# Landmark attention and two MLPs on one core: q by token parity, scores as eight 64x32 tiles, k and v in one product, and a new prologue order

## The chip, the core and the metric

The kernel runs on one core of one Trainium2 chip. The metric is the device time of the whole program in microseconds (us), the median of three runs. Engines are named as in the profile: PE (TensorE), DVE (VectorE), ACT (ScalarE), POOL (GpSimd) and SP (SyncE, which issues nearly all the loads and stores).

## What is computed

```python
a = softmax(phi, axis=2)                      # phi: 4 x 8 x 576 x 32
k_m = einsum('bhsm,bhsd->bhmd', a, k)         # 32 landmarks per head
v_m = einsum('bhsm,bhsd->bhmd', a, v)
attn = softmax(q @ k_m.T / 8)                 # 576 x 32 per head
x = (attn @ v_m), heads side by side          # 2304 tokens x 512
h = max(x @ w1, x @ w2, x @ w3)               # d_ff 768
x = h @ w_out
out = softplus(x @ m_in) @ m_out              # d_ff 2048, result 2304 x 512
```

q, k, v and phi are float32. The six weight matrices arrive as 64-bit words that the kernel turns into float32 itself.

## The kernel before

**Units.** The attention is done in eight units of one batch and four heads each (`units`); unit u has batch u // 2 and heads 0 to 3 or 4 to 7. A batch has 576 tokens, taken as four blocks of 128 and a remainder of 64 (`R4`, `SREM`). Units 0 to 3 belong to the first two batches and are worked off in the prologue; units 4 to 7 are worked off later, between the large products of the first two batches.

**The steps of a unit.** `load_phi`, `load_x` (k is i = 0, v is i = 1) and `load_q` bring the data in. `att_max` finds the largest phi of each landmark: three maxima on DVE, a product with the identity on PE that turns the 128x128 result, a row maximum, a diagonal matrix `md` and a product with ones that spreads it to all partitions. `att_exp` subtracts and exponentiates (`et`). `att_x` multiplies `et` with k or with v, for four heads side by side in four 128x32 tiles, and, the first time, `et` with a column of ones, which gives the sums of the softmax; `ri` is their reciprocal and `kvd` the normalised result. `att_tr` turns `kvd` by two products with a selection matrix (`pick2`), giving `kT` or the unit's part of v. `att_q` turns q with transposes on PE. `att_sc` multiplies `kT` with `qT`: for each half of the tokens (288 columns) two 128x64 tiles, the contraction running over two heads' 64 dimensions each. `att_sm0`, `att_sm1`, `att_sm2` and `att_fin` do the softmax over the landmarks on DVE, POOL and ACT, and split the result into a high and a low part (`ah`, `al`).

**The first MLP.** v_m and the three weight matrices are multiplied ahead (`u_step`, `u_mm`, `u_mr`: `uh`, `ul`), so that `m1_step` goes from attention weights to the maximum directly: 18 products of 288 columns for one block of 128 hidden units, one batch and one half of its tokens. `m1out` then multiplies with w_out. The weights w1 to w3 come in halves (`w_load`, three loads of 256 KB each) and are converted by `ca_step` or `conv`. All this is done for the first two batches and again for the last two; the second MLP (`m2in`, `m2out`) follows, and `m2out` writes rows of the result from SP.

**What sets the order.** The prologue's order is the hand-made list `PLAN`: each entry names a step and a unit, every step is a generator that is advanced by one `yield` per entry, and the engines keep the order of the list (`tc.manual_schedule`). After the plan a scheduler places the steps of `phase_a` and `phase_o`, and those of units 4 to 7 between them, by the slots in `C`. Each engine and SP's queue of transfers works in its order; a transfer whose buffer is still in use holds all transfers behind it on SP.

Of the kernel before, what the change touches and what calls it, by code (L numbers as in the profile page):

```python
# [68 lines left out]
    'us0': 1,  # L69
    'us1': 0,  # L70
# [3 lines left out]
def fused_kernel(ctx: ExitStack, tc: tile.TileContext, q, k, v, phi, w1, w2, w3, w_out, m_in, m_out, out):  # L74
# [63 lines left out]
    ones = const.tile([P, 2], F32, name="ones")  # L138
# [94 lines left out]

    def load_phi(u):
# [9 lines left out]
        nc.gpsimd.memset(ph[SREM:P, :, R4, :], 0.0)  # L244
        U[u]["ph"] = ph

    def load_x(u, i):
# [3 lines left out]
        if u in (2, 3):  # L251
            x = h_p.tile([P, 4, R4, D], F32, tag=f"h{2 * u - 1 - i}", name="kvm")
        else:
            x = t_p.tile([P, 4, R4, D], F32, tag=f"x{i}", name="kvm", bufs=2)
        if u in (2, 3):
            xr = wo_p.tile([SREM, 4, D], F32, tag=f"woh{2 * u - 2 + i}", name="kvr")
        else:
            xr = t_p.tile([SREM, 4, D], F32, tag=f"xr{i}", name="kvr", bufs=2)
# [5 lines left out]
    def load_q(u):  # L264
# [717 lines left out]
```

## Time and profile before

| | us |
|---|---|
| median of three runs (lowest, highest) | 730.91 (728.87, 731.75) |
| the profiled execution, whole | 731.49 |
| its span, first to last instruction | 729.7 |
| PE busy in the span | 699.0 (96%) |
| DVE, ACT, POOL busy | 410.7, 297.3, 250.9 |
| mean granted clock of PE | 0.986 of full speed |

The time to predict is that of the whole execution. PE is the busiest engine; what it does not work, and what it works at the lower of its two clock levels, stands mostly in the first 100 us, where the loads are also densest. A matmul's own duration in the trace includes the time in which the next ones already run, so what a group of matmuls costs PE is read from the start of its first to the start of what follows.

### The profile page before, as it was taken

What the parts mean: (1) busy time and instruction counts of PE and PEld (TensorE: products, weight loads), DVE (VectorE), ACT (ScalarE), POOL (GpSimd) and SP (SyncE); (2) the same over time, 40 slices, a digit from 0 to 9 for tenths busy, and PEclk for the clock granted to TensorE, in tenths of its full rate; (3) what the DMA queues carried; (4) which work ended last, traced back from release to release, by engine and by line L of the source; (5) the groups of instructions that cost most, each with busy time, mean ns of one, the idle gap of its engine ahead of it and who ended that gap; (6) DMA issues with size and microseconds to landing.
All of it is one profiled execution on the core that took longest, in us unless ns stands there. A gap on an engine that the chain in (4) does not pass through costs nothing. (4 is left out here: it accounts for less than half of the span.)

```text
span 729.7 us, 12242 instructions
## 1 busy us (share of the span) xinstructions
PE 699.0 (96%) x4680; PEld 614.9 (84%) x4680; DVE 410.7 (56%) x780; ACT 297.3 (41%) x628; POOL 250.9 (34%) x239
## 2 busy tenths in 40 slices
PE   6789999999979999989999999999999999999997
PEld 4466777888879999889988989989889899889895
DVE  4777885825689955772332685334783335333342
ACT  3454564437377734553233553222542224222221
POOL 1201233237384406842222452222542224222221
PEclk9889999999989999999999999999999999999999
DMA  8987975411234102530000231000340000011112
GB/s 194 260 266 213 284 215 163 121 33 51 69 99 142 50 1 78 152 118 1 1 0 1 59 116 57 1 1 0 90 143 1 0 1 1 0 44 44 44 49 81
DMA packets 70490, 59.25 MB, mean 81 GB/s; under 512 B 27936, under 2 KB 65312, under 8 KB 70432
## 3 DMA queue, kind: packets, MB, share of 16 engines
q1 hardware_dynamic: 70432, 58.47, 27.7%
q8 instruction: 37, 0.61, 0.3%
q14 instruction: 21, 0.17, 0.1%
HBM read 53.74 MB, written 4.72 MB: 80 GB/s over the span
## 5 line engine op out<-in xcount | busy, mean ns | idle before, releaser
L161 POOL TENSOR_TENSOR gl<-m,gh 128x384 fp32r<-128x384 f32 x96 | 100.5, 1048 | 253.7 <-ACT gh L153 237.6
L889 DVE TENSOR_SCALAR e<-pst 128x384 int32<-128x384 int32 x96 | 53.2, 555 | 134.4 <-PE pst L883 134.4
L891 ACT ACTIVATE L<-e 128x384 f32<-128x384 f32 x96 | 50.3, 524 | 184.8 <-DVE e L889 184.7
L915 PE MATMUL acc<-oh,gh 128*128 128x512 f32 x288 | 113.7, 395 | 0.4 <-ACT gh L153 0.4
L915 PE MATMUL acc<-ol,gh 128*128 128x512 f32 x288 | 113.4, 394 | 0.0
L883 PE MATMUL pst<-yb,ih 128*128 128x384 f32 x384 | 102.1, 336 | 0.0
L606 PE MATMUL psm<-ah,uh 128*128 128x288 f32 x288 | 89.9, 312 | 5.0 <-ACT mt L613 3.2
L606 PE MATMUL psm<-al,uh 128*128 128x288 f32 x288 | 86.8, 301 | 0.0
L606 PE MATMUL psm<-ah,ul 128*128 128x288 f32 x288 | 86.2, 301 | 0.3 <-DVE ul L562 0.3
L893 DVE SCALAR_TENSOR_TENSOR m<-pst,L 128x384 f32<-128x384 f32 x96 | 53.4, 556 | 55.9 <-ACT L L891 55.9
L915 PE MATMUL acc<-oh,gl 128*128 128x512 f32 x288 | 82.7, 394 | 0.0
L153 ACT ACTIVATE gh<-m 128x384 fp32r<-128x384 f32 x96 | 50.0, 523 | 63.4 <-DVE m L893 62.0
L883 PEld LDWEIGHTS pst<-yb,ih 128*128 128x128 f32 x384 | 70.0, 188 | 3.4 <-DVE m L893 0.7
L883 PE MATMUL pst<-y0h,ih 128*128 128x384 f32 x192 | 64.9, 338 | 2.7 <-DVE m L893 2.5
L606 PEld LDWEIGHTS psm<-ah,uh 128*128 128x128 f32 x288 | 55.7, 193 | 13.2 <-ACT mt L613 4.0
L883 PE MATMUL pst<-y0l,ih 128*128 128x384 f32 x192 | 64.5, 336 | 0.0
L883 PE MATMUL pst<-y0h,il 128*128 128x384 f32 x192 | 64.4, 336 | 0.0
L883 PE MATMUL pst<-yb,il 128*128 128x384 f32 x192 | 64.4, 335 | 0.0
L915 PEld LDWEIGHTS acc<-oh,gl 128*128 128x128 f32 x288 | 53.6, 187 | 11.4
L915 PEld LDWEIGHTS acc<-oh,gh 128*128 128x128 f32 x288 | 53.9, 187 | 10.5 <-ACT gh L153 0.9
L915 PEld LDWEIGHTS acc<-ol,gh 128*128 128x128 f32 x288 | 54.0, 187 | 8.9
L606 PEld LDWEIGHTS psm<-ah,ul 128*128 128x128 f32 x288 | 55.5, 193 | 1.2 <-issue 0.6
(152 smaller groups left out, 1323.1 us busy)
## 6 DMA issues: line engine op xcount, KB each, us to landing
wraw<-in_moe_w_dram SPq DMA_DIRECT2D x66, 256.0 KB, 3.8
raw<-in_moe_w_in_dram SPq DMA_DIRECT2D x16, 512.0 KB, 3.7
raw<-in_moe_w_out_dram SPq DMA_DIRECT2D x16, 512.0 KB, 3.7
out_dram<-o SPq DMA_DIRECT2D x18, 256.0 KB, 2.1
kvm<-in_k_dram SPq DMA_DIRECT2D x8, 512.0 KB, 5.3
kvm<-in_v_dram SPq DMA_DIRECT2D x8, 512.0 KB, 6.5
wor<-in_moe_w_out_dram SPq DMA_DIRECT2D x6, 512.0 KB, 3.7
ph<-in_phi_dram SPq DMA_DIRECT2D x8, 256.0 KB, 4.1
```

What stands on the lines that cost most here:

```text
L153: nc.scalar.activation(out=dst, in_=src, func=AF.Copy)
L161: return e.tensor_tensor(out=dst, in0=src, in1=hi, op=ALU.subtract)
L606: nc.tensor.matmul(x, l[:, t, ws], r[:, cs], start=(n == 0), stop=(n == 5))
L883: nc.tensor.matmul(hx, l[:, ds], r[:, cs], start=(n == 0), stop=(n == 3 * ND - 1))
L889: nc.vector.tensor_scalar(out=e.bitcast(I32), in0=hx.bitcast(I32), scalar1=0x7FFFFFFF, scalar2=None, op0=ALU.bitwise_and)
L891: nc.scalar.activation(out=L, in_=e, func=AF.Softplus, scale=-1.0)
L893: nc.vector.scalar_tensor_tensor(out=m, in0=hx, scalar=0.0, in1=L, op0=ALU.max, op1=ALU.add)
L915: nc.tensor.matmul(acc[0][t], l[:, t * P:(t + 1) * P], r, **kw)
```

## The change

The tokens of a batch are reordered: `qT` holds the even tokens of a block in partitions 0 to 63 and the odd ones in 64 to 127, so that q can be loaded in runs of four tokens (1 KB) in place of one (256 B), and so that the scores of a head have a contraction of 64. The result's rows are put back by the stores. `par` holds 1 or 0 by the parity of the head, and 1 in its last two columns; `ri` times `par` puts a head's v into the half of `kvd` that it belongs to, and one transpose then turns it. In units 4 to 7 k and v are one product (`att_x` with i = 2, 128 columns). The padding of phi and of the remainders makes all contractions 128 deep. Beside this, `PLAN` is a new list with nearly the same steps, and weight halves (1,0), (1,1), (2,0) and (3,1) get load buffers of their own.

```diff
@@ tiles and loads
-    pick2 = const.tile([P, 2, P], F32, name="pick2")
+    par = const.tile([P, 4], F32, name="par")
-        nc.gpsimd.memset(ph[SREM:P, :, R4, :], 0.0)
+        nc.gpsimd.memset(ph[SREM:P, :, R4, :], -3e38)
+        nc.gpsimd.memset(xr[SREM:P], 0.0)
@@ load_q
+        dma(out=x, in_=q[b, hs, 0:R4 * P, :].rearrange("h (p r) d -> p h (r d)", r=R4))
         for h in range(4):
-            dma(out=x[:, h // 2, :, (h % 2) * D:(h % 2 + 1) * D],
-                in_=q[b, 4 * g + h, 0:R4 * P, :].rearrange("(r p) d -> p r d", r=R4))
-        dma(out=xr, in_=q[b, hs, R4 * P:S, :].rearrange("h p d -> p h d"))
+            dma(nc.scalar if u in C["aq"] else nc.sync, out=xr[32 * h:32 * h + 32],
+                in_=q[b, 4 * g + h, R4 * P:S, :].rearrange("(p r) d -> p (r d)", r=2))
@@ att_max
-        nc.vector.tensor_tensor(out=m2, in0=ph[:, :, 0:2], in1=ph[:, :, 2:4], op=ALU.max)
-        nc.vector.tensor_tensor(out=mx, in0=m2[:, :, 0], in1=m2[:, :, 1], op=ALU.max)
-        nc.vector.tensor_tensor(out=mx[0:SREM], in0=mx[0:SREM], in1=ph[0:SREM, :, R4], op=ALU.max)
+        nc.vector.tensor_reduce(out=mx, in_=d["ph"].rearrange("p h r m -> p h m r"), op=ALU.max, axis=AX.X)
-        nc.tensor.matmul(st[:, 0:P], mx.rearrange("p h m -> p (h m)"), ident, start=True, stop=True)
+        nc.tensor.transpose(st[:, 0:P], mx.rearrange("p h m -> p (h m)"), ident)
+        if u < 4:
+            nc.scalar.activation(out=md, in_=ident, func=AF.Copy, scale=mc)
@@ att_exp
+        nc.gpsimd.tensor_tensor(out=es, in0=et[:, 0:2], in1=et[:, 2:4], op=ALU.add)
+        nc.gpsimd.tensor_tensor(out=es[:, 0], in0=es[:, 0], in1=es[:, 1], op=ALU.add)
+        nc.gpsimd.tensor_tensor(out=es[:, 0], in0=es[:, 0], in1=et[:, R4], op=ALU.add)
@@ att_x
-                nc.tensor.matmul(xp[a, 0:D], et[k, r, a], x[:, h, r] if r < R4 else xr[:, h], start=(r == 0), stop=(r == R4))
-                    nc.tensor.matmul(xp[a, D:D + 2], et[k, r, a], ones[k], start=(r == 0), stop=(r == R4))
+                nc.tensor.matmul(o[a], et[:, r, a], x[:, h, r] if r < R4 else xr[:, h], start=(r == 0), stop=(r == R4))
+            nc.tensor.matmul(xp[:, n:n + 4], d.pop("es"), ones, start=True, stop=True)
+            nc.vector.tensor_tensor(out=ri, in0=ri, in1=par, op=ALU.mult)
@@ att_tr
-        for s in range(2):
-            nc.tensor.matmul(st[64 * s:64 * s + 64, P:2 * P], kvd, pick2[:, s], start=True, stop=True)
+        nc.tensor.transpose(st, kvd, ident)
@@ att_sc
-        for c in range(2):
-            for s in range(2):
-                nc.tensor.matmul(sc[64 * s:64 * s + 64, 0:HS], kT[:, s ^ flip], qT[:, s ^ flip, c * HS:(c + 1) * HS],
-                                 start=True, stop=True)
+        for h in range(4):
+            a = slice(32 * (h ^ 2 * flip), 32 * (h ^ 2 * flip) + 32)
+            for c in range(2):
+                k = slice(64 * c, 64 * c + 64)
+                nc.tensor.matmul(sc[c][a, 0:HS], kT[k, 32 * h:32 * h + 32], qT[k, h], start=True, stop=True)
@@ w_load
-        t = a_p.tile([P, 2, 3, P, 2], I32, tag="wraw", name="wraw", bufs=2)
+        n = C["wr"].get((i, hf))
+        if n is None:
+            t = a_p.tile([P, 2, 3, P, 2], I32, tag="wraw", name="wraw", bufs=2)
+        else:
+            t = wo_p.tile([P, 2, 3, P, 2], I32, tag=f"wo{n}", name="wraw")
@@ m2out
-                    dma(out=out[r0:r0 + P, :], in_=O[ck, t])
+                    for p0, n, r0, st in rows(ck * CH + t * P):
+                        dma(out=out[r0:r0 + (n - 1) * st + 1:st, :], in_=O[ck, t][p0:p0 + n])
```

The list `PLAN` moves the loads. On SP, the first transfers before were these (`ph` is phi, `qn` and `qnr` q and its remainder, `kvm` and `kvr` k or v and its remainder, `wraw` a part of w1 to w3):

```order
L127 DMA ph<-in_phi_dram 128x4x128
L127 DMA ph<-in_phi_dram 64x4x32
L127 DMA ph<-in_phi_dram 128x4x128
L127 DMA ph<-in_phi_dram 64x4x32
L127 DMA qn<-in_q_dram 128x4x64 x4
L127 DMA qnr<-in_q_dram 64x4x64
L127 DMA kvm<-in_k_dram 128x4x256
L127 DMA kvr<-in_k_dram 64x4x64
L127 DMA qn<-in_q_dram 128x4x64 x4
L127 DMA qnr<-in_q_dram 64x4x64
```

With the change SP begins as follows:

```order
L133 DMA ph<-in_phi_dram 128x4x128
L133 DMA ph<-in_phi_dram 64x4x32
L133 DMA qn<-in_q_dram 128x4x256
L133 DMA kvm<-in_k_dram 128x4x256
L133 DMA kvr<-in_k_dram 64x4x64
L133 DMA ph<-in_phi_dram 128x4x128
L133 DMA ph<-in_phi_dram 64x4x32
L133 DMA wraw<-in_moe_w_dram 128x2x256 x3
L133 DMA qn<-in_q_dram 128x4x256
L133 DMA ph<-in_phi_dram 128x4x128
```

A unit's q is one transfer in place of four (its remainder, for units 0 and 1, is issued by ACT), k of unit 0 stands fourth in place of tenth, and the first weight half follows phi of unit 1. The last transfer for v of units 0 and 1 is the 27th on SP, in place of the 29th; q of unit 2 and the second weight half are now ahead of it, phi of unit 2 behind it.

On PE, unit 6 stood before between products of the first MLP (L606) like this (`kvm` and `kvr` are v, then k; `et` the exponentials):

```order
L606 MATMUL psm<-ah,uh 128x288
L324 MATMUL pst<-kvm,et 32x64 x16
L324 MATMUL pst<-kvr,et 32x64 x4
L330 MATMUL pst<-ones,et 32x2 x20
L324 MATMUL pst<-kvm,et 32x64 x16
L324 MATMUL pst<-kvr,et 32x64 x4
L606 MATMUL psm<-al,uh 128x288
```

With the change, the same place reads:

```order
L639 MATMUL psm<-ah,uh 128x288
L350 MATMUL pst<-kvm,et 32x128 x16
L350 MATMUL pst<-kvr,et 32x128 x4
L353 MATMUL pst<-ones,es 128x4
L300 MATMUL pst<-ident,mx 128x128
L639 MATMUL psm<-al,uh 128x288
```

Sixty products of 64 and 2 columns have become twenty of 128 columns and one of 4 (the row of L300 belongs to unit 7).

At SP's end the last three stores of 128 rows (o_5045, o_5047 and o_5049 before) have become these seven:

```order
L133 DMA out_dram<-o_4830 64x512
L133 DMA out_dram<-o_4830 32x512 x2
L133 DMA out_dram<-o_4832 96x512
L133 DMA out_dram<-o_4832 32x512
L133 DMA out_dram<-o_4834 96x512
L133 DMA out_dram<-o_4834 32x512
```

The parts of one tile go to rows that lie 2 or 4 apart.

## Rows read from the trace of the kernel before

**Rows 1.** Windows: us, busy us of each engine (instructions), granted clock, DMA share, GB/s.
```profile
0.00:20.00 20.00, 13.34 (x145) 9.32 (x149) 9.42 (x30) 5.85 (x11) 1.90 (x12) 1.00 0.83 199
20.00:40.00 20.00, 14.67 (x292) 9.59 (x282) 16.25 (x38) 10.52 (x24) 4.95 (x4) 0.83 0.99 276
40.00:60.00 20.00, 16.98 (x234) 10.90 (x232) 15.10 (x32) 8.61 (x22) 2.52 (x3) 0.83 0.78 220
60.00:80.00 20.00, 19.14 (x132) 15.76 (x131) 16.67 (x40) 11.21 (x28) 4.04 (x4) 1.00 0.92 253
80.00:100.00 20.00, 18.66 (x148) 15.08 (x147) 17.75 (x43) 10.00 (x24) 5.41 (x8) 1.00 0.92 265
100.00:120.00 20.00, 20.00 (x315) 15.85 (x314) 13.02 (x38) 10.61 (x31) 8.89 (x11) 1.00 0.61 183
```
**Rows 2.** Timeline of SP around its wait for a weight buffer: start, us, engine, line, what.
```profile
35.43 0.61 SPq L127 DMA_DIRECT2D kvr<-in_v_dram  x1
40.19 1.40 SPq L127 DMA_DIRECT2D wraw<-in_moe_w_dram  x3
```
**Rows 3.** Timeline of PE, first block of m1 (first and last product), end of the tenth.
```profile
37.83 0.40 PE L606 MATMUL psm<-ah,uh 128*128 128x288 f32 x1
...
40.18 0.29 PE L606 MATMUL psm<-ah,ul 128*128 128x288 f32 x1
...
87.90 0.29 PE L606 MATMUL psm<-ah,ul 128*128 128x288 f32 x1
```
**Rows 4.** Timeline of PE, unit 6: products of v, ones and k, and what follows.
```profile
139.49 0.65 PE L324 MATMUL pst<-kvm,et 128*32 128x64 f32 x32
...
140.32 0.60 PE L330 MATMUL pst<-ones,et 128*32 128x2 f32 x40
140.86 0.65 PE L324 MATMUL pst<-kvm,et 128*32 128x64 f32 x32
...
141.69 0.40 PE L606 MATMUL psm<-al,uh 128*128 128x288 f32 x1
```
**Rows 5.** Timeline of PE, two of the products of u, 384 columns in two tiles.
```profile
52.47 0.49 PE L555 MATMUL psm<-wh,v 128*64 128x384 f32 x1
...
52.80 0.49 PE L555 MATMUL psm<-wh,v 128*64 128x384 f32 x1
```
**Rows 6.** Timeline of PE, k_m and v_m of unit 6 turned, and four transposes of q.
```profile
144.79 0.66 PE L348 MATMUL pst<-pick,kvd 128*64 128x128 f32 x8
145.37 0.40 PE L606 MATMUL psm<-ah,ul 128*128 128x288 f32 x1
...
149.42 0.60 PE L397 MATMUL pst<-ident,qr 128*128 128x128 f32 x4
149.78 0.42 PE L652 MATMUL psm<-hlo,woh 128*128 128x384 f32 x1
```
**Rows 7.** Timeline of PE, q's remainder and one half of unit 4's scores.
```profile
134.44 0.33 PE L393 MATMUL pst<-ident,qr 64*128 64x64 f32 x2
134.71 0.40 PE L606 MATMUL psm<-ah,uh 128*128 128x288 f32 x1
...
135.17 0.71 PE L429 MATMUL pst<-qT,kT 128*64 128x288 f32 x4
135.80 0.40 PE L606 MATMUL psm<-ah,ul 128*128 128x288 f32 x1
```
**Rows 8.** Timeline of POOL and DVE, a POOL operation beside DVE's conversion of weights.
```profile
48.64 1.16 POOL L450 TENSOR_TENSOR sT<-sT,smx 128x576 f32<-128x576 f32 x1 [12.88 <-DVE smx L442]
48.79 1.42 DVE L197 SCALAR_TENSOR_TENSOR wh<-wraw,wh 128x384 int32<-128x384 int32 x1
50.52 0.56 DVE L197 SCALAR_TENSOR_TENSOR wl<-wraw,wl 128x384 int32<-128x384 int32 x1
```
**Rows 9.** Groups of POOL: line, operation, shapes, count, busy us, mean ns, idle before.
```profile
L161 POOL TENSOR_TENSOR wol<-cg,woh 128x256 fp32r<-128x256 f32 x12 | 9.0, 768 | 23.6 <-ACT woh L153 23.5
```
**Rows 10.** Timeline of SP at the end of the program: the last three stores.
```profile
725.39 1.53 SPq L127 DMA_DIRECT2D out_dram<-o  x3
```

More of the change, by code (lines that the diff above doesn't have):

```diff
@@ L137, in fused_kernel @@
     make_identity(nc, ident)
-    ones = const.tile([P, 2], F32, name="ones")
+    ones = const.tile([P, 4], F32, name="ones")
     nc.vector.memset(ones, 1.0)
@@ L232, in new_vT, with pre @@
             vT[pp] = tuple(a_p.tile([P, H, 64], F32R, tag=f"v{x}", name=f"v{x}") for x in "hl")
+    def pre(kind, u, i=0):
+        if "pre" not in CK:
+            CK["pre"] = wo_p.tile([P, 3 * DM], F32, tag="wo2", name="pre")
+        n, o = (4 * D, (2 * (u - 2) + i) * 4 * D) if kind == "kv" else (2 * D, 16 * D + u * 2 * D)
+        return CK["pre"][:, o:o + n]
     def load_phi(u):
@@ L252, in load_x @@
             x = h_p.tile([P, 4, R4, D], F32, tag=f"h{2 * u - 1 - i}", name="kvm")
+            xr = pre("kv", u, i).rearrange("p (h d) -> p h d", h=4)
         else:
[L254 to L258, printed above, removed]
+            if "x2" not in U[u]:
+                U[u]["x2"] = (t_p.tile([P, 2, 4, R4, D], F32, tag="x", name="kvm", bufs=2),
+                              t_p.tile([P, 2, 4, D], F32, tag="xr", name="kvr", bufs=2))
+            x, xr = (y[:, i] for y in U[u]["x2"])
         dma(out=x.rearrange("p h r d -> p h (r d)"),
                           in_=src[b, hs, 0:R4 * P, :].rearrange("h (p r) d -> p h (r d)", r=R4))
-        dma(out=xr, in_=src[b, hs, R4 * P:S, :].rearrange("h p d -> p h d"))
+        dma(out=xr[0:SREM], in_=src[b, hs, R4 * P:S, :].rearrange("h p d -> p h d"))
+        nc.gpsimd.memset(xr[SREM:P], 0.0)
         U[u]["x", i] = (x, xr)
@@ L303, in att_exp @@
         ph, ma = d.pop("ph"), d.pop("ma")
+        if u in C["exp"]:
+            mas = t_p.tile([P, 4, M], F32, tag="md", name="mas", bufs=2)
+            nc.scalar.activation(out=mas, in_=ma, func=AF.Copy)
+            ma = mas
+            yield
         e.tensor_tensor(out=ph, in0=ph, in1=ma.unsqueeze(2).to_broadcast([P, 4, R4 + 1, M]), op=ALU.subtract)
@@ L316, in att_x @@
         et = d["et"]
-        x, xr = d.pop(("x", i))
+        two = i == 2
+        if two:
+            x, xr = d.pop("x2")
+            x, xr = x.rearrange("p i h r d -> p h r i d"), xr.rearrange("p i h d -> p h i d")
+        else:
+            x, xr = d.pop(("x", i))
+        n = 2 * D if two else D
         xp = pst() if u >= 4 else psm()
-        new_ri = "ri" not in d
+        o = xp[:, 0:n].rearrange("p (i d) -> p i d", i=2) if two else xp[:, 0:n]
         for r in range(R4 + 1):
@@ L322, in att_x @@
                 a = slice(32 * h, 32 * h + 32)
-                k = slice(0, P if r < R4 else SREM)
-                nc.tensor.matmul(xp[a, 0:D], et[k, r, a], x[:, h, r] if r < R4 else xr[:, h], start=(r == 0), stop=(r == R4))
-        if new_ri:
-            for r in range(R4 + 1):
-                for h in range(4):
-                    a = slice(32 * h, 32 * h + 32)
-                    k = slice(0, P if r < R4 else SREM)
-                    nc.tensor.matmul(xp[a, D:D + 2], et[k, r, a], ones[k], start=(r == 0), stop=(r == R4))
+                nc.tensor.matmul(o[a], et[:, r, a], x[:, h, r] if r < R4 else xr[:, h], start=(r == 0), stop=(r == R4))
+        if "ri" not in d:
             yield
-            ri = t_p.tile([P, 1], F32, tag="ri", name="ri", bufs=2)
-            nc.vector.tensor_scalar(out=ri, in0=xp[:, D:D + 1], scalar1=1e-9, scalar2=None, op0=ALU.add)
+            nc.tensor.matmul(xp[:, n:n + 4], d.pop("es"), ones, start=True, stop=True)
+            yield
+            ri = t_p.tile([P, 4], F32, tag="ri", name="ri", bufs=2)
+            nc.vector.tensor_scalar(out=ri, in0=xp[:, n:n + 4], scalar1=1e-9, scalar2=None, op0=ALU.add)
             nc.vector.reciprocal(out=ri, in_=ri)
+            nc.vector.tensor_tensor(out=ri, in0=ri, in1=par, op=ALU.mult)
             d["ri"] = ri
         yield
-        kvd = t_p.tile([P, D], F32, tag="kvd", name="kvd", bufs=3)
-        nc.scalar.activation(out=kvd, in_=xp[:, 0:D], func=AF.Copy, scale=d["ri"])
-        d["xp", i], d["kvd", i] = xp, kvd
+        ri = d["ri"]
+        for j in (0, 1) if two else (i,):
+            kvd = t_p.tile([P, 2, D], F32, tag="kvd", name="kvd", bufs=4)
+            oj = o[:, j] if two else o
+            if j == 0:
+                nc.scalar.activation(out=kvd, in_=oj.unsqueeze(1).to_broadcast([P, 2, D]), func=AF.Copy, scale=ri[:, 2:3])
+            else:
+                for s in range(2):
+                    nc.scalar.activation(out=kvd[:, s], in_=oj, func=AF.Copy, scale=ri[:, s:s + 1])
+            d["xp", j], d["kvd", j] = xp, kvd.rearrange("p s d -> p (s d)")
     def att_tr(u, i):
@@ L391, in pe @@
             if s == 2:
-                for a in range(2):
-                    nc.tensor.transpose(qp[:, a * SREM:(a + 1) * SREM], xr[:, 2 * a:2 * a + 2].rearrange("p h d -> p (h d)"),
-                                        ident[0:SREM, 0:SREM])
-                return qp
-            for r in range(R4):
-                nc.tensor.transpose(qp[:, r * P:(r + 1) * P], x[:, s, r], ident)
+                nc.tensor.transpose(qp[:, 0:P], xr, ident)
+                return qp
+            for n in range(4):
+                nc.tensor.transpose(qp[:, n * P:(n + 1) * P], x[:, 2 * s + n // 2, n % 2 * P:(n % 2 + 1) * P], ident)
             return qp
@@ L424, in att_sc @@
         flip = units[u][0] % 2 if u >= 4 else 0
[L425 to L431 removed]
+        sc = [pst() if u >= 4 else psm() for c in range(2)]
+        for h in range(4):
[3 more added lines that the diff above has]
+                nc.tensor.matmul(sc[c][a, 0:HS], kT[k, 32 * h:32 * h + 32], qT[k, h], start=True, stop=True)
+        d["sc"] = sc
         yield
@@ L620, in wo_conv @@
     def wo_conv(j, **kw):
-        hi = wo_p.tile([P, DM], F32R, tag=f"woh{j}", name=f"woh{j}")
-        lo = wo_p.tile([P, DM], F32R, tag=f"wol{j}", name=f"wol{j}")
+        for x in (2 * j // 3, (2 * j + 1) // 3):
+            if ("wo", x) not in wo_t:
+                wo_t["wo", x] = wo_p.tile([P, 3, DM], F32R, tag=f"wo{x}", name=f"wo{x}")
+        hi, lo = (wo_t["wo", x // 3][:, x % 3] for x in (2 * j, 2 * j + 1))
         wr = a_p.tile([P, DM, 2], I32, tag="wor", name="wor", bufs=1)
@@ L902, in soft2, with rows @@
         G[n] = (gh, gl)
+    def rows(c0):
+        c, r = c0, []
+        while c < c0 + P:
+            n, j = divmod(c, HS)
+            k = min(x for x in (P, 2 * P, HS) if x > j)
+            m = min(k - j, c0 + P - c)
+            st = 4 if j < 2 * P else 2
+            r.append((c - c0, m, n // 2 * S + n % 2 + j // P * (2 if j < 2 * P else R4 * P // 2) + j % P * st, st))
+            c += m
+        return r
     def m2out(n):
```

63 lines of the change are left out of this document (34 added, 29 removed), and 56 rows, old and new, of the table PLAN.

## The prediction

> **What bounds the kernel now.** I read the windows of 20 us first, because PE's 96% is a mean over stages. In the first 100 us PE is busy 13.3, 14.7, 17.0, 19.1 and 18.7 of 20 us, from 100 us on 20.0 [rows 1]. So there are two stages. Up to about 88 us, where the tenth block of m1 ends [rows 3], PE waits for others: 17.2 us of the first 100 are idle. Part of what it does work there runs at the lower clock: a mean granted clock of 0.83 in two windows, made of the levels 1 and 0.5 (2.4 and 1.2 GHz), is 0.34 of 40 us at the low one, 13.6 us [rows 1]. From 100 to 200 us PE is the bound: every product taken away there shortens the kernel, as long as nothing else comes too late.
>
> What PE waits for in the prologue is read from the loads and the order, since PE's waits are short ones that follow from each other. In the first 60 us the transfers move 199, 276 and 220 GB/s, 13.9 MB in all, with DMA shares of 0.83 to 0.99 in the first two windows and 0.78 in the third [rows 1]. The third is low because SP issues nothing from 36.04 to 40.19: a weight transfer waits for its buffer, and all others behind it [rows 2]. The first block of m1 starts at 37.83 [rows 3] although its inputs (two whole units and one weight block, 5.7 MB) were only part of what had moved.
>
> **The change in the stage from 100 us on (units 4 to 7).** Each piece is priced from its start to the start of what follows.
>
> Product of k and v: now 0.83 us for one of them, 0.54 for the sums, 0.83 for the other, 2.20 in all [rows 4]. A product of 384 columns takes PE 0.33 us per pass, with its two tiles beside each other [rows 5]; a pass of 128 columns is 0.11. The new form has five rounds of four tiles and two passes (40 records for 20 products in rows 4): 5 x 2 x 0.11 = 1.1. If the 64-column rate of rows 4 were set by the number of instructions and not by columns, it would be 0.8; if the new columns cost double, 1.7. I take 1.1, the row with the longest columns being nearest to a stream. The sums on PE shrink to one product of 4 columns, some 0.1 (a whole 128-column transpose is 0.09 [rows 6]; the old sums, 0.54, are the upper end). Saving 1.0 per unit, 4.0 in all, with 2 and 5 as ends. Unit 4's twenty-plus products stood in nine places between others and stand in two now, unit 5's in three in place of one; a return costs about 0.15 (0.63 for a half of the scores [rows 7] less 0.48 of stream, below), so five or six fewer returns give 0.8.
>
> Turning k_m and v_m: 0.58 [rows 6] against two transposes of 0.09 each (four take 0.36 [rows 6]): 0.4 per unit, 1.6. q's remainder: 0.27 [rows 7] against one transpose of 0.09: 0.2 per unit, 0.7. The turned maxima: left at nothing, they are a matmul for a transpose.
>
> Scores: two halves of 0.63 [rows 7]; of each, 0.48 is stream (two passes of 288 columns at 0.33 per 384) and 0.15 the return. The new form has eight tiles of 64x32. If all eight run beside each other, as the two tiles in rows 5 do, two halves become 0.48 + 0.15: 0.63 saved per unit. No row shows tiles that share columns and differ in rows; if those run one after the other, only one return of 0.15 is saved. I take the first, but for three units only, because one unit's eight products stand in two places of four: 1.9, ends 0.4 and 2.5.
>
> The stage together: 4.0 + 0.8 + 1.6 + 0.7 + 1.9 = **9.0 us**, ends 5 and 11. Its cover: DVE is busy 13 of 20 us and POOL 9 of 20 from 100 to 120 us [rows 1]; a stage shorter by a tenth leaves them room.
>
> **The change in the prologue.** PE's own savings matter little while it waits; the order of loads decides. The new list has nearly as many transfers up to v of units 0 and 1 (27 for 29, at 0.61 us each [rows 2]), but they carry more: in place of q's four transfers of 128 KB one of 512. It has moved the second weight half ahead of v of units 0 and 1, and q of unit 2 with it; and the buffers of their own take away the wait of rows 2. The last load that holds PE's order is k of unit 2: in PE's list its product stands in front of m1 (1,0,1), the fourth block. Up to that load SP brings all four units (8.3 MB) and five weight halves (0.79 each): 12.2 MB. With the first 20 us as now (4.0 MB) and the rest at the 276 GB/s of the second window [rows 1], it has landed at 20 + 8.2 / 0.276 = 49.7 us.
>
> Behind it PE has seven blocks of m1 at 2.5 us (2.35 from the first to the last start and one pitch more [rows 3]), four steps of u at four passes of 0.33 [rows 5], 5.3; two products at 0.83 [rows 4], 1.7; scores and turns, 1.2: 25.7 us at the full clock. That is 75.4. I add 2.6 for softmax chains that come late (unit 2's scores are known only some 2 us after its k, and its transposes, subtraction, exponential and products pass DVE, POOL and ACT in turn before blocks (0,1) and (1,1) can start): 78.0 in place of 88.0, **10.0 us** won. Ends: all loads at 276 GB/s and no late chain, 44.2 + 25.7 = 69.9, 18 us won; loads at the mean of 232 of the three windows, 52.6, and 8 us of late chains or low clock, 86.3, 2 us won. By then m1 has ten blocks behind it in either kernel.
>
> Smaller edits on other engines: the maximum is one DVE operation in place of three, `md` goes to ACT, `ri` gets one multiplication more; they stand beside PE's work, together within 1 us of DVE per unit, and are left at nothing. ACT issues eight small q transfers: at 0.61 each, 4.9 us of ACT's first 20, where it is busy 5.9 [rows 1]; four of them stand before its first work and four between two evacuations of q. That is part of the ends above.
>
> **GpSimd's sums, and a rule that speaks against them.** POOL adds three sums per unit, of 256 and twice 128 elements: 0.77 for 256 [rows 9], so about 1.5 us per unit. While POOL's subtraction ran, from 48.64 to 49.80, DVE's conversion of the same shape took 1.42 us in place of 0.56 [rows 8]: 0.86 lost. The Trainium skill (SBUF — State Buffer, "Who interferes with whom") says that a VectorE instruction with two SBUF inputs contends with a GpSimd instruction that reads SBUF, and that the loser waits for the whole instruction. The rows agree with that, and by it each of the new sums may hold DVE once. In the sum I give this no term of its own: DVE has 3.8 to 4.9 us of 20 free between 20 and 60 us [rows 1], and four units' sums are 6 us over 75. If it decides, it is rival A.
>
> **The tail.** The last three stores take SP 1.53 us, 0.51 each, from 725.39 on [rows 10]. Now there are seven for the same three tiles: 7 x 0.51 = 3.6, so that the last is issued 2.0 us later. If a store of 32 rows is cheaper to issue in proportion, it is 0.5. I take 2.0: the issues of other sizes (0.61 for a remainder, 0.47 for each of the three of 256 KB at 40.19 [rows 2]) do not follow size.
>
> **Sum.** 731.5 (the profiled execution) - 9.0 - 10.0 + 2.0 = 714.5. The median of the runs lies 0.6 below that execution: 713.9, **714 us**. The ends of its terms give 704 (11 and 18 won, 2 lost, 0.6 off: 703.9) to 726 (5 and 2 won, 2 lost, 0.6 off: 725.9).
>
> **Rivals.**
> A. The prologue wins nothing, because DVE or POOL takes the place of the loads. For it: DVE is busy 15 to 18 of 20 us from 20 to 100 us [rows 1]; a prologue of 78 us would need nearly the same work in 10 us less; twelve new sums, each holding DVE for 0.86, would be 10.3 us, just what was won. Against it: the sums are spread out and DVE is often idle for its inputs. Time: 731.5 - 9.0 + 2.0 - 0.6 = 724.
> B. The stage from 100 us on does not give its 9 us, because the eight tiles run in two rows after each other (1.5 less) and the evacuations on ACT or the weights come late now that PE reaches them sooner; DMA shares of 0.92 up to 100 us [rows 1] speak for the latter. With half of the stage's gain: 718.5.
> C. Slower: the new order of loads backfires. Phi of unit 3, q of unit 2 and the second weight half now stand in front of v of units 0 and 1, all of it on one queue, and no block of m1 can start without v. If the loads then move less than now, the k of unit 2 comes late and 25.7 us of PE's work behind it. The kernel is slower by over 0.5% (3.7 us) from a loss of 10.7 us in the prologue on (9.0 and 2.0 set off): k at 88.0 + 10.7 - 25.7 - 2.6 = 70.4 us, that is, 12.2 MB at under 173 GB/s. At 150 GB/s it would be at 81.3, the tenth block at 109.6, and the kernel at 746 us. For it stands only the 199 GB/s of the first window, for longer runs of q against it 276 and 253 in the others [rows 1].
> D. The change doesn't reach the time: PE's saved work becomes waits elsewhere, and the kernel stays at 731.
>
> **How the numbers follow.** Forecast 0.58; A 0.17; B 0.19; C 0.03; D 0.03. What a measurement can tell from no change is 0.5%, 3.7 us, so 727.3 to 734.6 is "same". Forecast, A and B are faster, C slower, D the same: 0.94, 0.03, 0.03. The range reaches from 704 to A with tiles that run in two rows (724 + 1.5) and to the far end of the terms, 726, rounded up: 727; it leaves out C, D and the edge of B with A, under 0.1, and what the terms may have missed.
>
> **What would show it.** Right: from 100 to 200 us PE at 20.0 of 20 still; eight score products from start to the next product 0.6 to 0.7 us; the joint product 1.1 to 1.3; two turns 0.2; the first block of m1 near 33 us, the tenth block done at 76 to 80; SP without a gap at 36 to 40; DMA over 250 GB/s from 20 to 60 us; seven stores in 3.6 us at the end. Wrong: the tenth block after 86 us (A or C, told apart by whether DVE or the loads are busy then); PE idle in the stage after 100 us (B); eight tiles that take over 1 us.

## The result, and the profile after

723.93 us, median of four runs (723.3 to 724.62), against 730.07 for the kernel before (728.87 to 731.75): a ratio of 0.9915, 95% interval 0.989 to 0.994. The change wins 6.1 us; the forecast was 714.0, some 17 us. The range of 704 to 727 holds the result. The profiled execution took 723.56 us, with a span of 721.7.

Windows of PE over four stages, cut where the tenth block of m1 ends, where the second half's m1 starts, and where that half's first output product starts. First the kernel before (us, length and busy us, granted clock, DMA share, GB/s):
```profile
0.00:88.03 88.03, 70.82 (x831) 0.92 0.90 240
88.03:200.06 112.03, 112.03 (x1128) 1.00 0.42 116
200.06:276.84 76.78, 72.71 (x494) 0.96 0.22 70
276.84:725.10 448.26, 443.41 (x2234) 1.00 0.14 42
```
The same of the changed kernel:
```profile
0.00:79.13 79.13, 62.09 (x677) 0.94 0.76 211
79.13:185.43 106.30, 102.30 (x803) 1.00 0.56 164
185.43:265.02 79.59, 74.28 (x510) 0.94 0.21 67
265.02:715.17 450.15, 445.13 (x2234) 1.00 0.14 42
```
Read them as differences: the prologue is 8.9 us shorter (forecast 10.0), the second stage 5.7 (forecast 9.0, of products alone), the second half's m1 is 2.8 us **longer** and the rest 1.9 longer (both forecast at nothing). Behind the last product the span goes on for 6.5 us instead of 4.6 (forecast 2.0 more, seen 1.9). In sum -8.0, the difference of the spans. The second row says where to look: before, PE was busy for all of its 112.03 us, now for 102.30 of 106.30. PE had 9.7 us less to do there (0.6 of it because unit 7's scores now stand behind 185.43) and waits for 4.0.

Of the signs that the forecast named, the first block of m1 starts at 36.30 us (forecast near 33), and the loads run at 274 and 243 GB/s from 20 to 60 us (forecast over 250 in both).

The pieces are what the forecast priced. Timeline of PE in the changed kernel: unit 4's scores, unit 6's joint product with its sum, one half turned, each with the start of what follows (the counterparts of [rows 4, 6, 7]):
```profile
129.63 0.71 PE L459 MATMUL pst<-qT,kT 64*32 64x288 f32 x16
130.27 0.40 PE L639 MATMUL psm<-ah,ul 128*128 128x288 f32 x1
...
133.51 1.08 PE L350 MATMUL pst<-kvm,et 128*32 128x128 f32 x32
134.41 0.40 PE L350 MATMUL pst<-kvr,et 128*32 128x128 f32 x8
134.74 0.39 PE L353 MATMUL pst<-ones,es 128*128 128x4 f32 x2
134.98 0.31 PE L300 MATMUL pst<-ident,mx 128*128 128x128 f32 x1
...
141.28 0.27 PE L379 MATMUL pst<-ident,kvd 128*128 128x128 f32 x1
141.31 0.42 PE L686 MATMUL psm<-hh,wo 128*128 128x384 f32 x1
```
All eight score tiles together take 0.64 us, as long as one half did [rows 7]: they run beside each other. k and v take 1.23 (forecast 1.1), the sum's product 0.24 (forecast 0.1), a turn 0.03 here until the next product starts (0.25 at 106.77 us).

**The new waits.** SP's timeline has one merged row of 15 weight transfers that lasts 32.52 us. Three waits stand in it, the counterpart of the gap in [rows 2]:
```profile
42.21 32.52 SPq L133 DMA_DIRECT2D wraw<-in_moe_w_dram  x15
74.84 1.74 SPq L131 DMA_DIRECT2D wraw<-in_moe_w_dram  x3
76.64 1.12 SPq L131 DMA_DIRECT2D ph<-in_phi_dram  x2
```
SP's waits from 40 to 80 us, the longest line (what it waited for, us in total, times, longest):
```profile
SPq L133 <- DVE wl L204: 20.0, 3, 11.4
```
In the kernel before, phi of unit 4 was issued here:
```profile
67.46 1.13 SPq L125 DMA_DIRECT2D ph<-in_phi_dram  x2
```
The windows of the same stretch, in the columns of [rows 1]:
```profile
40.00:60.00 20.00, 16.85 (x236) 11.39 (x236) 17.99 (x38) 10.34 (x28) 5.24 (x6) 1.00 0.85 243
60.00:80.00 20.00, 18.80 (x131) 15.99 (x127) 16.88 (x37) 9.23 (x23) 5.03 (x6) 1.00 0.31 93
```
The queue wait of [rows 2] was taken away at 36 to 40 us, and a longer one stands at 62 to 74: w(4,0), issued at 57.20, and w(4,1), at 73.33, wait for buffers that VectorE has not read yet, and phi, v and k of unit 4 stand behind them. DMA falls to 93 GB/s, and phi of unit 4 is issued at 76.64 us, 2.5 us before the tenth block ends; before, it was issued 20.6 us ahead of that end. So VectorE's row maxima of the later units (L297) come between the returns of m1 and u, at 1.35 and 1.26 us each:
```profile
83.14 1.35 DVE L297 TENSOR_REDUCE mx<-ph 128x128 f32<-128x640 f32 x1 [0.15 <-DMA ph<-in_phi_dram]
...
88.88 1.26 DVE L297 TENSOR_REDUCE mx<-ph 128x128 f32<-128x640 f32 x1 [1.17 <-DMA ph<-in_phi_dram]
```
and PE, which never stood still from 88.03 to 200.06 us before, now waits, mostly for VectorE (timeline of PE, idle before the row in brackets):
```profile
85.64 0.40 PE L639 MATMUL psm<-ah,uh 128*128 128x288 f32 x1 [0.63 <-DVE mt L648]
...
90.20 0.33 PE L300 MATMUL pst<-ident,mx 128*128 128x128 f32 x1 [0.67 <-DVE mx L297]
...
103.04 0.51 PE L569 MATMUL psm<-wh,v 128*64 128x384 f32 x1 [0.78 <-DVE ul L574]
...
145.57 0.66 PE L426 MATMUL pst<-ident,qr 128*128 128x128 f32 x4 [1.07 <-DVE ph L323]
...
195.84 0.53 PE L639 MATMUL psm<-ah,uh 128*128 128x288 f32 x2 [1.00 <-ACT ah L504]
...
197.42 0.61 PE L639 MATMUL psm<-al,uh 128*128 128x288 f32 x1 [1.05 <-DVE al L168]
...
209.34 0.45 PE L608 MATMUL psm<-wh,vh 128*128 128x384 f32 x1 [2.02 <-DVE mt L648]
```
Only one of the first four waits for a maximum itself; that the others come from the late loads too can't be read from these rows; run 2 tests it. The last three are in the second half's m1. PE comes to it at 185.43 instead of 200.06 us, 14.6 earlier, but unit 7's softmax is done only some 7 us earlier. Its last step on DVE, before:
```profile
203.18 0.75 DVE L161 TENSOR_TENSOR al<-aT,ah 128x576 fp32r<-128x576 f32 x1
```
The same with the change, and one long step of a weight conversion behind it:
```profile
196.62 0.75 DVE L168 TENSOR_TENSOR al<-aT,ah 128x576 fp32r<-128x576 f32 x1
...
203.02 1.08 DVE L203 TENSOR_SCALAR cg<-cg 128x384 int32<-128x384 int32 x1
```
Around these waits the granted clock falls too: 5.32 us of work are done in 194 to 202 us at a mean of 0.65, which costs an estimated 1.9 us beside the idle 2.7 (0.35 of the 5.32), and 3.71 us in 210 to 214 at 0.57:
```profile
194.00:202.00 8.00, 5.32 (x21) 0.65 0.49 149
...
210.00:214.00 4.00, 3.71 (x17) 0.57 0.85 261
```

### The profile page after: what moved, and what is told of

Read it like the earlier page. It is cut to its first block, busy times and chain, and to the rows that moved or that the text cites. A ratio compares the mean times of both kernels' runs of the same rounds, so it can differ in the third digit from the quotient of the medians.

```text
span 721.7 us, 11376 instructions
## 1 busy us (share of the span) xinstructions
PE 683.8 (95%) x4216; PEld 606.2 (84%) x4216; DVE 416.9 (58%) x764; ACT 299.9 (42%) x640; POOL 269.8 (37%) x283
## 5 line engine op out<-in xcount | busy, mean ns | idle before, releaser
L961 PE MATMUL acc<-oh,gl 128*128 128x512 f32 x288 | 82.8, 396 | 0.0
L639 PEld LDWEIGHTS psm<-al,uh 128*128 128x128 f32 x288 | 55.8, 194 | 1.7 <-DVE al L168 1.7
```

The source lines that it names most:

```text
L639: nc.tensor.matmul(x, l[:, t, ws], r[:, cs], start=(n == 0), stop=(n == 5))
L961: nc.tensor.matmul(acc[0][t], l[:, t * P:(t + 1) * P], r, **kw)
```

## The experiments

Times are medians, each beside runs of the kernel before (729.6 to 730.4 us); in brackets stand the ratio to those and its 95% interval. The changed kernel's ratio is 0.9915 (0.989 to 0.994), so a difference of 1 or 2 us between two runs whose intervals overlap is not clear of the noise. A profile is of one execution, and in runs 1, 3, 5, 9 and 12 that execution lies 1.7 to 4.5 us above the median. My theory: PE's work went as priced, and it is given back by the late loads of unit 4, by unit 7's softmax, and by the stores. The rivals: the sums on GpSimd (rival A), VectorE's own work, or chance.

**1. Whole blocks stored** (the result's rows then stay in the order of the parity split).
```
-  for p0, n, r0, st in rows(ck * CH + t * P):
-      dma(out=out[r0:r0 + (n - 1) * st + 1:st, :], in_=O[ck, t][p0:p0 + n])
+  dma(out=out[ck * CH + t * P:ck * CH + (t + 1) * P, :], in_=O[ck, t])
```


> The changed kernel with the 18 stores of the second pass as whole contiguous blocks again (output rows then stand in the order of the parity split, so they are permuted). Theory (tail = 2.0 us of stores, forecast and seen as 9.9 us won at the last product but 8.0 at the span's end): 723.9 - 2.0 = 722 us, the last product unmoved at about 715 us into the span and the span's end 7.0 us behind... no: 6.5 us behind it less 2.0 = 4.5 us behind it. Rival (the end costs nothing, the 1.9 us is chance of the clock): 724 us, span's end still 6.5 us behind the last product. This run is a second profile of everything ahead of the tail too: if the clock of 0.57 in 312 to 316 us belongs to the program, it is there again; if it was chance, it isn't.

721.75 us (0.9896, 0.9879 to 0.9914), 2.2 less than the changed kernel by the medians; the intervals overlap. The profile shows the end apart from the rest. SP's timeline at the end, of the changed kernel and then of this one, to hold against [rows 10]:
```profile
715.46 3.45 SPq L133 DMA_DIRECT2D out_dram<-o  x7
```
```profile
718.32 1.53 SPq L133 DMA_DIRECT2D out_dram<-o  x3
```
Behind the last product the span goes on for 4.6 us (718.03 to 722.6), as in the kernel before, instead of 6.5: the tail's term of 2.0 is right. The low clock behind 312 us came again (0.57 from 316 to 320).

**2. Unit 4's loads ahead of w(4).**
```
-    ('wl', 4, 0),
+    ('ph', 4), ('ld', 4, 1), ('ld', 4, 0), ('wl', 4, 0),
...
-    bg[0].append(lambda: (new_vT(1), load_u(4)))
+    bg[0].append(lambda: new_vT(1))
```


> The changed kernel with the loads of unit 4 (phi, v, k) issued ahead of the two weight loads w(4,0) and w(4,1) instead of behind them. Theory (SP's queue holds these loads until 74.7 us behind buffers that VectorE has not read, so the row maximum of unit 4 comes after the returns of m1 need VectorE): phi of unit 4 issued near 62 us instead of 76.64, PE's gaps between 84 and 104 us (3.9 us in all) shrink to under 1.5 us, the second half's m1 starts 2 to 3 us before 185.4, time 721 to 722. Rival (the gaps are VectorE's own work, the maximum over 128x640 at 1.3 us and the conversions, and come whenever the unit comes): gaps move but stay 3 to 4 us in sum, time 724. Rival (w(4,0), w(4,1) come later by the 1.5 MB moved ahead and m1 of block 4 waits for them): time 726.

719.85 us (0.9867, 0.9853 to 0.9881), 4.1 less than the changed kernel by the medians, 3.5 by the ratios. Windows of PE:
```profile
0.00:82.38 82.38, 61.72 (x678) 0.96 0.81 232
82.38:183.80 101.42, 100.83 (x800) 1.00 0.51 148
183.80:262.63 78.83, 72.33 (x510) 0.96 0.22 68
```
Phi of unit 4 is issued at 54.16 us, and PE idles 0.6 us of the second stage instead of 4.0: the theory. Its prologue is 3.3 us longer; unit 4's first maximum and three more waits of PE (0.42 to 0.84 us) now stand in it. So PE comes to the second half's m1 1.6 us earlier, m1 is 0.8 shorter, and what follows 1.5: this execution doesn't have the stretch of low clock behind 312 us. Of what is won, the next wait takes a part:
```profile
197.81 0.85 PE L639 MATMUL psm<-ah,uh 128*128 128x288 f32 x2 [5.36 <-ACT ah L504]
```

**3. Scores and softmax of units 5 to 7 due earlier.**
```
-  'scs': [[-8, -7, -7, -6, -5, 0], [-6, -4, -4, -3, -2, 1], [-1, 0, 1, 2, 3, 4], [2, 4, 4, 5, 6, 8]],
+  'scs': [[-8, -7, -7, -6, -5, 0], [-7, -6, -6, -5, -4, -2], [-4, -3, -3, -2, -1, 0], [-1, 0, 1, 2, 3, 4]],
```


> The changed kernel with the due slots of units 5, 6 and 7 of the scores and softmax moved ahead (unit 5 by 1, unit 6 by 3, unit 7 by 3 to 4 slots of some 2.7 to 4 us). Theory (after the change unit 7's softmax, ending 196.6 us, is later than PE's arrival at the second half's m1, 185.4, and PE waits 0.47 + 1.00 + 1.05 + 0.46 us between 193 and 200 us and then runs at a clock of 0.5 to 0.8): unit 7's scores some 8 us before 185, its al ready before PE asks for it, these gaps gone and the clock at 1.00 in 194 to 202: time 721 us. Rival (PE is held by its own work there and the gaps only move to the copies of u and h behind them): time 724 us.

723.43 us (0.9918, 0.9892 to 0.9943; runs from 720.46 to 726.56): a miss. In the profiled execution (726.07) the second half's m1 took 75.9 us instead of 79.6, but PE came to it at 191.8: in 170 to 175 us it waited 1.93 and 0.47 us for copies of qT on ScalarE and then ran at a clock of 0.50 (174 to 179 us). The wait moved.

**4. The new operations in the old order** (the list of before; what the new operations add stands right behind its step).
```
-    ('ph', 0), ('q', 0), ('ld', 0, 0), ('mx', 0), ('mx', 0), ('mx', 0), ('ph', 1), ('qT', 0), ('mx', 0),
...
+    ('ph', 1), ('ph', 0), ('q', 0), ('mx', 1), ('mx', 1), ('mx', 0), ('ld', 0, 0), ('mx', 1), ('mx', 1),
...
```


> The changed kernel's operations in the prologue's order of before (the steps that the new operations add stand right behind the step they belong to). Theory (the prologue's 8.8 us come two thirds from the order of loads, one third from PE work): the tenth block of m1 ends at 84 to 87 us instead of 79.2, the rest of the kernel as in the changed kernel less what the loads of unit 4 cost it there, time 727 to 730. Rival (the operations alone win it): 79 to 81 us for the tenth block, time 723 to 725. Rival (with the earlier loads of unit 4 that the old order has, the gaps of 84 to 104 us are gone, and all is given back and more): time 721.

723.2 us (0.9915, 0.9901 to 0.9929): the time of the changed kernel. Windows of PE:
```profile
0.00:89.81 89.81, 66.33 (x700) 0.92 0.88 253
89.81:190.00 100.19, 100.19 (x795) 1.00 0.37 114
190.00:266.29 76.29, 70.57 (x494) 0.96 0.22 70
266.29:715.08 448.79, 443.56 (x2234) 1.00 0.14 42
```
This splits the change in two. The operations alone (with the new form of q's loads and the buffers of their own) take 11.8 us out of the second stage, with PE busy throughout (some 0.7 of it because 22 of unit 4's 40 product records already stand before the tenth block), and make the prologue 1.8 us longer. The new order then makes the prologue 10.7 us shorter, and gives back 6.1 in the second stage, 3.3 in the second half's m1 and 1.4 behind it: nothing is left. My expectation of 727 to 730 was wrong. In this order phi of unit 4 is issued at 60.59 us, and there is a single wait, in the second half:
```profile
206.10 0.58 PE L832 MATMUL psm<-ah,uh 128*128 128x288 f32 x1 [5.72 <-DVE ul L812]
```

**5. Units 4 and 5 both ahead of w(4)** (as 2, with ('ph', 5), ('ld', 5, 1), ('ld', 5, 0) behind unit 4's, and load_u(5) gone from the slots).

> The changed kernel with the loads of units 4 and 5 both ahead of w(4,0) and w(4,1). With unit 4's alone the time fell from 723.4 to 719.9 us and the gaps of 78 to 180 us from 3.9 to 1.4; the largest gap left, 5.36 us to 197.8, waits on ScalarE's ah of unit 7. Theory (the loads of the later units set when their chains end): unit 7's scores come about 2 to 3 us ahead of the second half's m1 instead of 2 us behind its start, the gap of 5.4 shrinks to 3 to 4, time 718. Rival (unit 5 was early enough, and what is late is the chain of q loads and softmax steps, one unit behind the other): unit 7's scores stay at 185 to 186 us, time 720. Rival (w(4) now comes too late): time 723 or more.

719.23 us (0.9856, 0.9826 to 0.9887; runs from 717.04 to 723.77). Unit 7's scores stand before the second half's m1, whose largest wait is 1.91 us; but PE comes to it at 189.96. With both units' loads ahead the new order's lead in the prologue is gone: the last product of the tenth block starts at 90.25 us here, at 87.04 and 90.46 in runs 7 and 12 with the same prologue, at 89.1 to 89.7 in the old order (runs 4, 8, 11). Without these loads ahead it starts at 79.0 to 80.3 (the changed kernel and runs 1, 3, 6, 10), with unit 4's alone at 82.0 to 82.8 (runs 2, 9, 13, 14).

**6. The splits of the first half's output, one behind each block.**
```
-  nc.scalar.activation(out=t0, in_=xs[0], func=AF.Copy)
+  MT[i, 2 * bl + c] = nc.scalar.activation(out=t0, in_=xs[0], func=AF.Copy).ins
...
+  with tc.issue_after(MT[NJ + (3 + n) // 4, (3 + n) % 4]):
       cast("act", y0[dm][0][:, cs], y[:, cs])
```


> The changed kernel with the twelve splits of the first half's output (y0h on ScalarE, y0l on GpSimd) queued one behind each block of the second half's m1, instead of all twelve as soon as they can start (GpSimd 199.96 to 213.75 us without a pause). Theory: VectorE's conversions in 202 to 213 us (L203 1.08 to 1.22 us instead of 0.35 while GpSimd runs) are short again, PE's wait of 2.02 us to 209.3 goes, the clock is not at 0.57 in 210 to 214, the waits of 193 to 200 us (unit 7's softmax) stay: second half's output product 1.5 to 3 us earlier, time 721 to 722. Rival (the wait comes from the order on VectorE and not from its neighbour): time 723 to 724.

724.54 us (0.9912, 0.9890 to 0.9935; runs from 720.85 to 725.0): a miss in time. The wait of 2.02 us is 0.48 now, but the wait for unit 7's softmax ahead of it is unchanged (ah 1.02, al 1.04), waits of 0.69, 0.34 and 0.75 us for ul have come or grown, and the second half's m1 is as long as before the edit, 79.60 us.

**7 and 8. Edits 5 and 6, and edits 4 and 6, each with the stores on two queues**
```
+  dma(nc.scalar if x % 2 else nc.sync, out=out[r0:r0 + (n - 1) * st + 1:st, :], in_=O[ck, t][p0:p0 + n])
```


> Three edits on the changed kernel: loads of units 4 and 5 ahead of w(4), the splits of the first half's output spread over the blocks, and the output's stores issued in turn from SP's and ScalarE's queues. If the three losses are separate: 719 (loads) less 1.5 to 2.5 (spread) less 1 (the last seven stores in two queues instead of one) = 715 to 717 us. If the spread only moves the wait to unit 7's softmax: 718 to 719 us. If stores on ScalarE's queue hold its copies of gh in the last stretch: the last product later by 1 us or more, 720 us.

> The prologue in the order of before, with the spread of the first half's output splits and the stores on two queues. The old order alone gave 723.2 us, no gap from 90 to 200 us and one of 5.72 us to 206.1, ahead of which ScalarE copied seven y0h (3.00 us) before the conversions that VectorE then did in 1.2 us each. Theory (that gap is made by the splits): gap under 2 us, time 718 to 719. Rival (the gap is unit 7's softmax or the conversions themselves): gap 4 us or more, time 722.

718.24 us (0.9835, 0.9811 to 0.9859) and 717.62 (0.9827, 0.9802 to 0.9852). In run 8 the second half's m1 takes 71.56 us instead of 76.29, with one wait of 1.33 left in place of 5.72: that wait was made by the splits, which stood on ScalarE ahead of the weight conversions. In run 7 it takes 75.86. Behind the last product the span goes on for 6.0 us in both: the two queues win 0.5 of the 1 us expected.

**9. Unit 7's softmax without its row maximum, on run 2.**
```
+  if u not in (7,):
       nc.vector.tensor_reduce(out=mx, in_=sT, op=ALU.max, axis=AX.X)
...
+  if "mx" in d:
       e.tensor_tensor(out=sT, in0=sT, in1=d.pop("mx").to_broadcast([P, NJB, 32]), op=ALU.subtract)
```


> The kernel with unit 4's loads first (719.9 us), and in it unit 7's softmax without its row maximum and the subtraction of it (two VectorE steps of 0.73 and 1.38 us there; the quotient is the same without them). Nothing else is left out. Theory (the 5.36 us gap to 197.8 us is the length of unit 7's softmax chain past PE's arrival): the gap shrinks by 2 to 2.5 us to about 3, ah of unit 7 is there at 195 instead of 197.1, time 717.5 to 718.5. Rival (the gap is set by the conversions and copies of the second half's weights, which wait in the same queues): gap still 5 us, time 719.5 to 720.

722.68 us (0.9908, 0.9890 to 0.9926), slower than run 2: a miss. The chain was shorter and its waits shrank from 5.36 us to 0.63 + 1.75 (and 0.99 for ul), as expected, but then PE met the next one:
```profile
196.60 0.40 PE L641 MATMUL psm<-al,uh 128*128 128x288 f32 x1 [1.75 <-DVE al L168]
...
209.47 0.69 PE L610 MATMUL psm<-wh,vh 128*128 128x384 f32 x1 [3.02 <-DVE mt L650]
```
Run 2 had only 0.29 us of waiting at this place: with the softmax shorter, PE ran into the wait that stands among the splits in the changed kernel (2.02 us, run 6). Runs 13 and 14 test the two together.

**10. The sums of exponentials on TensorE.**
```
-  nc.gpsimd.tensor_tensor(out=es, in0=et[:, 0:2], in1=et[:, 2:4], op=ALU.add)
...
-  nc.tensor.matmul(xp[:, n:n + 4], d.pop("es"), ones, start=True, stop=True)
+  for r in range(R4 + 1):
+      nc.tensor.matmul(xp[:, n:n + 4], es[:, r], ones, start=(r == 0), stop=(r == R4))
```


> The changed kernel with the sums of exponentials as five accumulating 128x4 products on TensorE instead of three additions on GpSimd and one product. Theory (the sums on GpSimd cost PE little: one wait of 1.11 us at 50.4 and one of 0.3, and one 0.24 us product a unit): PE work up by 0.5 to 0.8 us a unit where it is the bound, three waits on es gone: time 723 to 727. Rival (GpSimd's additions, sharing with VectorE, are what holds VectorE in 40 to 120 us, the forecast's rival A): VectorE steps of 1.0 us and more in 40 to 120 us become rare, gaps of 78 to 180 us under 2 us in sum, time 720 or less.

726.15 us (0.9961, 0.9945 to 0.9977), 2.2 slower than the changed kernel. Groups of PE by line (busy us, mean ns, idle before), of the changed kernel and of this one:
```profile
L353 PE MATMUL psm<-ones,es 128*128 128x4 f32 x8 | 2.0, 314 | 1.4 <-POOL es L332 1.4
L353 PE MATMUL pst<-ones,es 128*128 128x4 f32 x8 | 1.5, 263 | 0.0
```
```profile
L351 PE MATMUL psm<-ones,et 128*128 128x4 f32 x40 | 5.9, 275 | 0.0
L351 PE MATMUL pst<-ones,et 128*128 128x4 f32 x40 | 5.1, 255 | 0.0
```
7.5 us more of the products' own durations, which overlap, against 1.4 us of waiting for GpSimd: the sums are well placed on GpSimd. Without them on GpSimd, VectorE still has nine steps of 1 us and more between 40 and 120 us (eleven in the changed kernel), and PE's waits from 78 to 180 us sum to 3.6 us (4.0): rival A falls.

**11 and 12. Runs 8 and 7 without the row maxima of units 4 to 7** (edit 9 with `u not in (4, 5, 6, 7)`).

> The old prologue order with the spread of the first half's output splits and stores on two queues (717.6 us), and units 4 to 7 without the row maximum and its subtraction (the quotient is the same without them). Theory (with the splits spread, the second half's m1 still waits 1.9 us, and the chain of unit 7 is what is left): 715 to 716.5 us. Rival (there PE is the bound all the way, and VectorE and GpSimd work comes free): 717 to 718 us.

> Loads of units 4 and 5 ahead of w(4), spread splits, stores on two queues (718.2 us), and units 4 to 7 without the row maximum and its subtraction (the quotient is the same without them). Theory (as for the old order): the wait of 1.90 us to 197.7 goes, 715.5 to 717 us. Rival (PE is the bound): 718 us.

716.41 us (0.9824, 0.9805 to 0.9844) and 716.25 (0.9811, 0.9787 to 0.9834), the lowest medians of all: both beat the kernel before by 13 us and the changed one by 7.5. Against runs 8 and 7 the ratios gain 0.0003 and 0.0024, within the noise. The second half's m1 in run 11:
```profile
190.36:261.60 71.24, 69.02 (x493) 1.00 0.24 75
```
Without low clock and with 2.2 us of waiting it takes 71.24 us; the changed kernel spends 79.59 on it. The two orders end alike again, and run 12's prologue is as long as the old order's:
```profile
0.00:90.30 90.30, 67.69 (x722) 0.91 0.88 241
```

**13 and 14. The lead kept: edits 2 and 6 with the stores of 7; then without row maxima too.**

> The new prologue order with unit 4's loads first, the spread of the first half's output splits and the stores on two queues, softmax whole. With unit 4's loads first alone (719.9 us) PE came to the second half's m1 at 183.8 us and then waited 5.36 us for unit 7's softmax. Theory (unit 7's chain stands in the way whenever PE comes before some 190 us, so a lead of the prologue past that is not to be had): PE again at 184, waits of 4 to 5.5 us for ah and al of unit 7, then no further wait: 717 to 718.5 us, no better than with units 4 and 5 first (718.2) or with the old order (717.6). Rival (the splits on GpSimd and ScalarE were what made unit 7's chain late): wait under 3 us, 714 us.

> The same, and units 4 to 7 without the row maximum and its subtraction (the quotient is the same without them). If unit 7's chain is the only thing between PE's lead and the end, the wait shrinks by some 2 us and the time is 714 to 715.5 us, 1 to 2 below the 716.3 us of both orders with the same edits: then the new order is worth that much. If the new order has nothing to give, 716 to 717 us.

720.13 us (0.9859, 0.9844 to 0.9874) and 716.69 (0.9814, 0.9792 to 0.9836). Run 13 missed its 717 to 718.5; it waits 5.35 us for ah again, so the splits don't make that chain late. On run 2 (719.85) neither the shorter softmax (run 9, 722.68) nor the spread splits (run 13, 720.13) won anything, and both together with the softmax of units 4 to 6 shortened too (run 14) won 3.2 us, 0.5 of it by the stores: the next chain stands right behind the one that is taken away. Run 14, by windows of PE:
```profile
82.00:184.74 102.74, 101.97 (x801) 1.00 0.50 147
184.74:260.85 76.11, 72.23 (x510) 0.98 0.22 70
```
PE comes to the second half's m1 5.6 us before run 11 and leaves it 0.75 before. The lead is spent there, on unit 7's scores and on waits for al and ul.

## Why the prediction was wrong

The sum came to 714.5 for the profiled execution, which took 723.56, 9.1 more. The prologue has 1.1 of this, the stage behind it 3.3, the second half's m1 2.8 and what follows 1.9.

- **The prologue's term, 10.0, was right as a number (8.9) and wrong as a gain.** The order of loads did decide it: k of unit 2 is multiplied at 48.23 us (forecast: landed at 49.7), and from there to the tenth block's end PE takes 30.9 us (forecast 28.3). Run 4 shows what the 8.9 is made of: 10.7 by the order, less 1.8 for the operations, for which the prediction had no term here. By "then m1 has ten blocks behind it in either kernel" I took the lead for time won. It was work put later: the new order has units 4 and 5 still to load and to prepare when the old one has them in hand, and with these loads back ahead of w(4) the lead is gone (run 5). In three pairs (723.9 and 723.2; 718.2 and 717.6; 716.3 or 716.7 and 716.4) the new order ends where the old one does. With unit 4's loads alone ahead, which keeps part of the lead, it is 3.4 us faster than the old one (run 2 against 4) and, with the splits spread in both, 2.5 us slower (run 13 against 8, intervals that overlap at their ends): the lead is worth what the next chain lets through.
- **The stage's term, 9.0, was too small for the products (about 11 in run 4) and had no wait in it.** The joint product and its sum are not where the surplus lies (2.20 less 1.47 is 0.7 per unit, forecast 1.0); which products or returns make it up isn't shown. The step that failed is "Its cover: ... a stage shorter by a tenth leaves them room". Busy shares from 100 to 120 us say nothing of when the inputs come: VectorE had room and still came late, since phi of unit 4 landed late: with its loads ahead (run 2), 3.4 of the 4.0 us of waiting in this stage are gone. Rival B had the size of this loss (4.5 of 9.0; 3.3 measured) but not the mechanism: the eight tiles do run beside each other, and what came late were the loads of the next units and the row maxima behind them.
- **No term for the second half's m1.** The kernel before already had one wait of 3.21 us there, ahead of 213.94 us, and a stretch of low clock behind it (0.50 from 214 to 218 us); I read the profile up to 200 us only. With work taken out ahead of a chain that ends when it ends, this stage grew by 2.8 us: 1.2 more of waiting, 0.6 for unit 7's scores, and the rest goes with the lower clock (0.94 instead of 0.96).
- **Queue waits move.** I priced the wait of [rows 2] as gone and didn't follow the same queue to its next shared buffer, w(4,0).
- **The tail, 2.0, was right** (run 1). **Rival A**'s time, 724, is what was measured, but by luck: the prologue did win 8.9 us, and its mechanism was refuted by run 10. C and D fell by the time.
- **The 1.9 us behind 265 us** had no term either. An estimated 1.6 of them are a stretch at a clock of 0.53 (312.5 to 316 us) behind a wait of 2.17 us. The kernel before has a wait as long there (2.09 us), and full clock. Behind that wait it came again in runs 1, 3, 5, 6, 8 and 9, and not in runs 2, 4, 7 and 10 to 14 (in run 14 the wait is 1.30 us); what decides it stays open.

## What to carry to other kernels

A step that is moved ahead wins time only if what PE needs next doesn't come later for it. Here the loads of units 4 and 5 were the price of the lead, and moved back ahead they cost all of it. Follow each queue past the wait that was removed, to the loads of the stage behind, and ask what PE does with its lead when it gets there. Where a stage with PE always busy is shortened, list the chains that end in it (softmax, conversions, splits) with the time at which each is done, since the first that isn't earlier becomes the new end; and expect to need several edits at once, because each alone may only move the wait (runs 9 and 13 against 14).

## What the runs showed of the hardware

- Eight tiles of 64x32 (16 records) take 0.64 us where two of 128x64 (4 records) took 0.63 [rows 7], the case for which no row of before stood: tiles that share columns and differ in rows run beside each other too. The Trainium skill (TensorEngine Tiling (Array Packing), "Available Configurations") lists 64x32 as eight independent tiles; the trace agrees.
- A product with 128 columns of weights and 4 of data takes 0.24 us (134.74 to 134.98), and five in a row take 1.13 in run 10 (98.72 to 99.85), while a transpose with 128 columns of data takes 0.09 [rows 6]: a narrow product is far dearer than its columns.
- A wait can cost more than its length: from 194 to 202 us PE was idle for 2.7 us, and the lower clock (a mean of 0.65) cost an estimated 1.9 more. It need not: run 11's 71.24 us with a longest wait of 1.36 stayed at 1.00, and so did the kernel before behind its wait of 2.09 us at 324.
- While GpSimd ran y0l without a pause (199.96 to 213.75 us), VectorE's shift of 128x384 (L203), which has one input, took 1.08 and 1.18 us instead of 0.35 (at 193.40); in the forecast I had looked at operations with two. The kernel before shows it too (1.19 and 1.15 us from 210.19 on), so it is no cost of the change. The Trainium skill (SBUF — State Buffer, "Who interferes with whom") names `tensor_scalar` among the operations that can enter the modes which use both port pairs, and so can contend with GpSimd; these rows agree. GpSimd's row:

```profile
199.96 13.79 POOL L168 TENSOR_TENSOR y0l<-ya,y0h 128x384 fp32r<-128x384 f32 x12 [0.76 <-POOL wl L168]
```
